# Feed-forward slices taken two at a time, with the weights' lower parts multiplied on 64 rows

## The chip, the core and the metric

The kernel runs on one core of a Trainium2 chip. The metric is the device time of one execution in microseconds (us), and what counts is the median over several executions. Five engines work side by side: TensorE (PE in the profile, its weight loads PEld), VectorE (DVE), ScalarE (ACT), GpSimd (POOL) and SyncE (SP, which here issues the DMA transfers). Each works through its own list of instructions in order and waits on semaphores for the others.

## The reference

An attention by way of 49 agents in each of 4 batches, and behind it a feed-forward with a sigmoid gate:

```python
# q, k, v: (4, 12480, 128); agents: (4, 49, 128); w_in: (128, 2048); w_out: (2048, 128)
a2k = sm(agents, k)                      # softmax over the keys, scale 1/sqrt(128)
agent_v = a2k @ v                        # (49, 128) in each batch
q2a = sm(q, agents)                      # softmax over the 49 agents
x = (q2a @ agent_v).reshape(49920, 128)
h = x @ w_in
out = (h * (1 / (1 + exp(-1.702 * h)))) @ w_out
```

## The kernel before, in words

`agent_weights` multiplies `agent_v` and `w_in` once for each batch, so that the up projection of the feed-forward is a product of the 49 softmax weights of a token with a matrix of 49 rows and 2048 columns. To keep precision beyond one pass of TensorE, numbers are held as a sum of two parts, a high one (rounded to the type `fp32r`) and a low one, the rest. The matrix becomes `wh` and `wl`. Its 49 rows stand twice in it, at partitions 0 to 48 and at 64 to 112 (`H` = 64).

Tokens go in groups of 960 (`GT`), 13 groups (`NG`) in each of 4 batches: 52 groups. A group has two chunks of 480 tokens (`CH`), and for each chunk `query_pairs` makes one tile of 128 partitions, which holds both parts of the softmax weights. In `sa` (chunk 0) the high parts lie at partitions 0 to 63 and the low parts at 64 to 127. In `sb` (chunk 1) it is the other way round: low parts at 0 to 63, high parts at 64 to 127. One matmul of `wh` with `sa` on 128 rows so sums high times high and high times low.

The hidden width of 2048 is cut in 16 slices of 128 (`NF`). A step `t` of the main loop is one slice of one group:

- `up` makes four matmuls into two PSUM banks `ph` (pool `ps_h`, four banks, so two slices' worth): `wh` with `sa`, `wh` with `sb` (line 362), then `wl` with `sa`, `wl` with `sb` (line 364). ACT then computes two gelus into `g` (line 369; three buffers). `gh`, the rounded copy of `g`, is made by ACT in even slices (`HI_ON_ACT`, line 371) and by DVE in odd ones (line 373), and DVE subtracts for `gl` (line 374). `gh` and `gl` have `LAG + 1`, five, buffers.
- `down`, for the slice four steps back (`LAG` = 4), makes six matmuls with `wo_h` and `wo_l` (line 385) that accumulate over the 16 slices in two banks `po`. Behind the last slice `store` copies them out by ACT and issues two DMAs on SP.

Around this, at fixed steps of each group, stand the side jobs: loads of queries, keys and values, the splitting of keys and queries into bfloat16 parts by POOL (lines 167 to 169), the scores (lines 182 to 189), the softmax of the next group's queries (line 328 is its exponential on ACT, with a table load before it and one back for the gelu), their transposes (line 345), and, for the next batch, key scores, their maximum (`key_max`, with transposes at lines 235 and 241), exponentials and the sum over values (`key_matmuls`, line 272). `beside` lists the jobs for the next batch. They are written ahead of the `up` of their step.

The order written is not quite the order that runs: a planner goes through the program when it is built, with costs of its own for each instruction, and may put an instruction that it holds ready ahead of one that it holds blocked. So in some slices the four up matmuls don't stand in a row.

Of the kernel before, what the change touches and what calls it, by code (L numbers as in the profile page):

```python
# [8 lines left out]
F32 = mybir.dt.float32  # L9
F32R = mybir.dt.float32r  # L10
# [3 lines left out]
AF = mybir.ActivationFunctionType  # L14
# [3 lines left out]
P = 128  # L18
TB = 120
KB = 8  # L20
CH = 480
GT = 2 * CH
LAG = 4
# [14 lines left out]
HI_ON_ACT = (0, 2, 4, 6, 8, 10, 12, 14)  # L38
# [4 lines left out]
def kernel(  # L43
# [10 lines left out]
    nc = tc.nc  # L54
# [3 lines left out]
    NF = F // P  # L58
    NG = N // GT
    NKG = N // (TB * KB)  # L60
    H = P // 2
# [7 lines left out]
    gpool = ctx.enter_context(tc.tile_pool(name="gpool", bufs=3))  # L69
    ps_h = ctx.enter_context(tc.tile_pool(name="ps_h", bufs=4, space=bass.MemoryType.PSUM))  # L70
    ps_o = ctx.enter_context(tc.tile_pool(name="ps_o", bufs=1, space=bass.MemoryType.PSUM))
    ps_m = ctx.enter_context(tc.tile_pool(name="ps_m", bufs=2, space=bass.MemoryType.PSUM))

# [1 line left out]
    ag_sb = const.tile([P, B, A], F32, name="ag_sb")  # L75
    nc.sync.dma_start(out=ag_sb, in_=agT)

    ident = const.tile([P, P], F32, name="ident")
    make_identity(nc, ident)
    # sel[k, m] = 1 where k and m name the same agent in either half  # L80
    sel = const.tile([P, P], F32, name="sel")
    nc.vector.memset(sel, 0.0)
    for c in range(2):
        nc.vector.tensor_add(
            out=sel[:, c * H : c * H + A], in0=ident[:, 0:A], in1=ident[:, H : H + A]
# [5 lines left out]
    for i in range(2):  # L91
        t = const.tile([P, KB, P], F32R, name=f"e_pair{i}")
        nc.gpsimd.memset(t.bitcast(F32), 0.0)
        e_pair.append(t)
        t = const.tile([P, KB, 2 * C + 2], F32R, name=f"v_pair{i}")
        nc.gpsimd.memset(t[:, :, 2 * C :].bitcast(F32), 1.0)
        v_pair.append(t)
        t = const.tile([P, CH // TB, P], F32, name=f"p_pad{i}")
# [7 lines left out]
    part_max = const.tile([P, NKG, A], F32, name="part_max")  # L106
    max_b = const.tile([P, A], F32, name="max_b")

    # a float64's words, low then high, to the nearest float32; what is under
    # float32's range becomes zero and what is over it infinite  # L110
    def load_words(src, i):
        w = loads.tile([P, 512, 2], U32, name="words", tag="kv")
        nc.sync.dma_start(out=w.rearrange("p n w -> p (n w)"), in_=src[:, i * 1024 : (i + 1) * 1024])
# [2 lines left out]
    def to_float32(w, out=None):  # L116
        lo = w[:, :, 0]
        hi = w[:, :, 1]
        ts = nc.vector.tensor_scalar
        stt = nc.vector.scalar_tensor_tensor  # L120
        # 2 ** exponent, with the sign
        tmp = work.tile([P, 2, 512], U32, name="tmp", tag="rest")
        ex = tmp[:, 0].bitcast(I32)
        ts(out=ex.bitcast(U32), in0=hi, scalar1=20, scalar2=0x7FF, op0=ALU.logical_shift_right, op1=ALU.bitwise_and)
        ts(out=ex, in0=ex, scalar1=1023 - 127, scalar2=1023 + 128, op0=ALU.max, op1=ALU.min)
        ts(out=ex, in0=ex, scalar1=float(127 - 1023), scalar2=float(1 << 23), op0=ALU.add, op1=ALU.mult)
        stt(out=ex.bitcast(U32), in0=hi, scalar=0x80000000, in1=ex.bitcast(U32), op0=ALU.bitwise_and, op1=ALU.bitwise_or)
        # the mantissa's upper 45 bits as a whole number, rounded once
        m = work.tile([P, 512], U32, name="m21", tag="o")
        r = tmp[:, 1]  # L130
        ts(out=m, in0=hi, scalar1=0xFFFFF, scalar2=0x100000, op0=ALU.bitwise_and, op1=ALU.bitwise_or)
        ts(out=r, in0=lo, scalar1=8, scalar2=None, op0=ALU.logical_shift_right)
        stt(out=m.bitcast(F32), in0=m, scalar=float(1 << 24), in1=r, op0=ALU.mult, op1=ALU.add)
        if out is None:
            out = m.bitcast(F32)
        stt(out=out, in0=m.bitcast(F32), scalar=2.0**-44, in1=ex.bitcast(F32), op0=ALU.mult, op1=ALU.mult)
        return out
# [7 lines left out]
        nc.scalar.copy(out=wo_h[:, s, :], in_=wo)  # L145
        nc.vector.tensor_sub(out=wo_l[:, s, :], in0=wo, in1=wo_h[:, s, :].bitcast(F32))

    # ---- scores: a float32 is the sum of three bfloat16, and of the parts'
    # products all are summed but those under a float32 product's own rounding ----
    ag_part = const.tile([P, B, 3, A], BF16, name="ag_part")  # L150
    rest = ag_sb
    for i in range(3):
# [7 lines left out]
        w = t.bitcast(BF16).rearrange("p (n w) -> p n w", w=2)  # L160
        return w[:, :, 1], w[:, :, 0]

    # the upper half of a word is the first part; of what is left the upper
    # half is the second, and the third takes the place of the lower
    def split(t):
        r = work.tile([P, GT + PAD], F32, name="rest", tag="rest")
        nc.gpsimd.memset(t[:, GT:], 0.0)  # L167
# [23 lines left out]
                nc.scalar.copy(out=o, in_=s[:, :, 0, :])  # L191
                nc.vector.tensor_add(out=o, in0=s[:, :, 1, :], in1=o)

# [1 line left out]
    def key_load(b, g):  # L195
        t = loads.tile([P, GT + PAD], F32, name="kt", tag="kv")
        nc.sync.dma_start(out=t[:, 0:GT], in_=kT[b, :, g * KB : (g + 1) * KB, :].rearrange("p j t -> p (j t)"))
        return t

    def first_key_scores(g, kt):  # L200
        # two batches' agents to a pass, as many columns as keep the clock up
        for c in range(2):
            ps = ps_m.tile([P, 512], F32, name="ps_m")
            for j in range(KB // 2):
                nc.tensor.matmul(  # L205
                    out=ps[:TB, j * 2 * A : (j + 1) * 2 * A],
                    lhsT=kt[:, c * KB // 2 + j, :],
                    rhs=ag_sb[:, 0:2, :].rearrange("p b a -> p (b a)"),
                    start=True,
                    stop=True,  # L210
                )
            s = ps[:TB, : KB * A].rearrange("p (j b a) -> p j b a", b=2, a=A)[:, :, 0, :]
            i = 2 * g + c
            nc.scalar.copy(out=score[:TB, i * KB // 2 : (i + 1) * KB // 2, :], in_=s)
        nc.vector.tensor_reduce(
            out=part_max[:TB, g, :],
            in_=score[:TB, g * KB : (g + 1) * KB, :].rearrange("p j a -> p a j"),
            axis=AX.X,
            op=ALU.max,
        )  # L220
# [87 lines left out]
            nc.vector.tensor_sub(out=wl[:, s], in0=pw, in1=wh[:, s].bitcast(F32))  # L308
        return wh, wl

# [1 line left out]
    def query_load(b, g):  # L312
        t = loads.tile([P, GT + PAD], F32, name="qt", tag="qt", bufs=2)
        nc.sync.dma_start(out=t[:, 0:GT], in_=qT[b, :, g * GT : (g + 1) * GT])
# [38 lines left out]
        nc.vector.tensor_sub(out=sb[0:H], in0=ps[H:P, :CH], in1=sb[H:P].bitcast(F32))  # L353
        return sa, sb

# [1 line left out]
    def up(f, wts, pairs):  # L357
        wh, wl = wts
        s = slice(f * P, (f + 1) * P)
        ph = [ps_h.tile([P, 512], F32, name="ph") for _ in range(2)]  # L360
        for c in range(2):
            nc.tensor.matmul(out=ph[c][:, :CH], lhsT=wh[:, s], rhs=pairs[c], start=True, stop=False)  # L362
        for c in range(2):
            nc.tensor.matmul(out=ph[c][:, :CH], lhsT=wl[:, s], rhs=pairs[c], start=False, stop=True)  # L364
        g = gpool.tile([P, 2, CH], F32, name="g")
        gh = gpool.tile([P, 2, CH], F32R, name="gh", bufs=LAG + 1)
        gl = gpool.tile([P, 2, CH], F32R, name="gl", bufs=LAG + 1)
        for c in range(2):
            nc.scalar.activation(out=g[:, c, :], in_=ph[c][:, :CH], func=AF.Gelu_apprx_sigmoid)  # L369
        if f in HI_ON_ACT:  # L370
            nc.scalar.copy(out=gh, in_=g)  # L371
        else:
            nc.vector.tensor_copy(out=gh, in_=g)  # L373
        nc.vector.tensor_sub(out=gl, in0=g, in1=gh.bitcast(F32))  # L374
        return gh, gl

    def down(f, gp, po):
        gh, gl = gp
        for lhsT, rhs, first, last in (
            (wo_h, gh, True, False),  # L380
            (wo_h, gl, False, False),
            (wo_l, gh, False, True),
        ):
            for c in range(2):
                nc.tensor.matmul(  # L385
                    out=po[c][:, :CH],
                    lhsT=lhsT[:, f, :],
                    rhs=rhs[:, c, :],
                    start=(f == 0 and first),
                    stop=(f == NF - 1 and last),  # L390
                )
# [5 lines left out]
            t0 = b * N + g * GT + c * CH  # L397
            nc.sync.dma_start(out=outT[:, t0 : t0 + CH], in_=o)

# [1 line left out]
    kts = {}  # L401
    vts = {}
    qts = {}
# [4 lines left out]
    wts = {}  # L408
    pairs = {}
# [41 lines left out]
    def do_weights(b):  # L451
        wts[b] = agent_weights(accs.pop(b))

    # the first batch's keys and values have nothing to run beside, and lie
    # where the weights and the hidden values come to lie afterwards
    def first_keys():
        tags = [("g", 3), ("gh", LAG + 1), ("gl", LAG + 1)]
        tiles = []
# [17 lines left out]
    words = [load_words(w_out, i) for i in range(NF // 4)]  # L476
# [7 lines left out]
    for g in range(NKG):  # L484
# [3 lines left out]
        for j in range(KB):  # L488
            nc.tensor.matmul(
                out=acc_ps[:A, : C + 1],  # L490
                lhsT=score[:TB, g * KB + j, :],
                rhs=vt[:TB, j, :],
                start=(g == 0 and j == 0),
                stop=(g == NKG - 1 and j == KB - 1),
# [10 lines left out]
    do_weights(0)  # L505
    down_weights(0, words[0])

    # what is done for the next batch beside a group: in steps of the group's
    def beside(b, g):
        jobs = {}  # L510
        if b == 0 and g == 0:
# [25 lines left out]
    steps = B * NG * NF  # L537
    live = {}
    po = {}
    for t in range(steps + LAG):  # L540
        n, f = divmod(t, NF)
        if t < steps:
            b, g = divmod(n, NG)
            if f == 0:
                jobs = beside(b, g)
            if f == 0:
                do_query_load(n + 2)
                if n == 0:
                    do_query_split(1)
            if f == QS_AT:  # L550
                do_query_split(n + 2)
            if f == Q_AT:
                do_query_scores(n + 1)
            if f == E_AT:
                do_query_softmax(n + 1)
            for job in jobs.get(f, ()):
                job()
            if f == P_AT:
                do_query_pairs(n + 1)
            live[t] = up(f, wts[b], pairs[n])  # L560
            if f == NF - 1:
                pairs.pop(n)
        if t >= LAG:
            n, f = divmod(t - LAG, NF)
            if f == 0:
                po[n] = [ps_o.tile([P, 512], F32, name=f"po{c}") for c in range(2)]
            down(f, live.pop(t - LAG), po[n])
            if f == NF - 1:
                store(*divmod(n, NG), po.pop(n))

# [37 lines left out]
```

## Time and profile before

| | |
|---|---|
| median of 3 runs | 2139.7 us (2138.86 to 2140.49) |
| span of the profiled execution | 2139.6 us, 0.1 under the median |
| mean granted clock of TensorE | 0.992 |
| PE busy | 2083.2 us (97%) |
| PE weight loads busy | 1777.1 us (83%) |
| DVE busy | 1865.0 us (87%) |
| ACT busy | 1611.9 us (75%) |
| POOL busy | 519.8 us (24%) |
| HBM | 50 GB/s over the span |

The profile is of one execution. It gives no time of that execution apart from its span, from the first instruction to the last, so the span stands for its own time. Matmuls follow one another as in a pipeline, and the ends of their records are modelled: a busy PE may still have room, and the distance between the starts of two matmuls is the surer measure. A row of a group gives the line, the engine, the operation, output and inputs with their shapes, and the count; behind the bar stand the busy time, the mean of one in ns, and the idle time just before them with what ended it. A row of the timeline gives start and duration in us, engine, line and operation; in brackets stand the idle time before it and what ended that.

### The profile page before, as it was taken

How to read it: one execution, taken by the hardware profiler on the slowest of the kernel's cores; microseconds unless marked ns; L12 is line 12 of the kernel's file. 1: busy time of each engine (PE TensorE's matmuls, PEld its weight loads, DVE VectorE, ACT ScalarE, POOL GpSimd, SP SyncE). 2: the span in 40 equal slices, each digit the busy share in tenths (PEclk: the TensorE clock that was granted, in tenths of full speed). 3: DMA queues.
4: the chain of work that ended last, by engine and by line, in shares of the span. 5: the costliest groups of instructions: out<-in, count | busy, mean ns of one | idle time of the engine just before them, and what ended most of it. 6: DMA issues, size and time to landing. Idle time of an engine off the chain costs nothing.

```text
span 2139.6 us, 31613 instructions
## 1 busy us (share of the span) xinstructions
PE 2083.2 (97%) x12232; PEld 1777.1 (83%) x12232; DVE 1865.0 (87%) x2142; ACT 1611.9 (75%) x2590; POOL 519.8 (24%) x383
## 2 busy tenths in 40 slices
PE   8889989999999999999999999999999999999999
PEld 8678878888888887788888888778888888888887
DVE  6998998999889899899888899899898887888876
ACT  3567768977777776987777777798777877778786
POOL 4143445121123433421113342531110101001000
PEclk9999999999999999999999999999999999999999
DMA  9411221211111212112101212111100101010000
GB/s 265 119 48 49 65 73 38 61 48 50 38 38 47 66 47 56 47 56 56 56 20 47 63 49 56 55 51 53 47 19 19 38 19 38 19 38 20 25 14 19
DMA packets 49339, 108.57 MB, mean 51 GB/s; under 512 B 4252, under 2 KB 30172, under 8 KB 49188
## 3 DMA queue, kind: packets, MB, share of 16 engines
q1 hardware_dynamic: 49188, 106.55, 17.2%
q8 instruction: 96, 1.57, 0.3%
q14 instruction: 55, 0.45, 0.1%
HBM read 80.97 MB, written 25.56 MB: 50 GB/s over the span
## 4 chain that ended last, share of the span: by engine, by line
PE 81%; DVE 11%; issue 3%; ACT 3%; POOL 1%; DMA 1%; ACTq 0%; SPq 0%; DVEq 0%; POOLq 0%
PE po L385 43%; PE ph L362 15%; PE ph L364 14%; DVE gl L374 5%; DVE gh L373 2%; PE ps_m L272 1%; PE ps_m L182 1%; PE ps_m L184 1%; POOL score L251 1%; PE ps_m L205 1%; ACT g L369 1%; PE ps_m L345 1%; PE ps_m L306 1%; PE ps_m L183 1%; PE ps_m L185 1%
## 5 line engine op out<-in xcount | busy, mean ns | idle before, releaser
L374 DVE TENSOR_TENSOR gl<-g,gh 128x960 fp32r<-128x960 f32 x832 | 1034.4, 1258 | 189.4 <-ACT gh L371 174.3
L369 ACT ACTIVATE g<-ph 128x480 f32<-128x480 f32 x1664 | 855.2, 573 | 380.5 <-PE ph L364 265.7
L385 PE MATMUL po<-gl,wo_h 128*128 128x480 f32 x1664 | 501.9, 382 | 5.4 <-DVE gl L374 5.4
L385 PE MATMUL po<-gh,wo_h 128*128 128x480 f32 x1664 | 506.1, 383 | 0.7 <-ACT gh L371 0.7
L385 PE MATMUL po<-gh,wo_l 128*128 128x480 f32 x1664 | 501.6, 383 | 0.0
L371 ACT CAST gh<-g 128x960 fp32r<-128x960 f32 x416 | 416.0, 1000 | 10.9
L385 PEld LDWEIGHTS po<-gl,wo_h 128*128 128x128 f32 x1664 | 313.1, 189 | 60.0 <-DVE gl L374 9.2
L385 PEld LDWEIGHTS po<-gh,wo_h 128*128 128x128 f32 x1664 | 313.5, 189 | 53.2 <-ACT gh L371 1.1
L385 PEld LDWEIGHTS po<-gh,wo_l 128*128 128x128 f32 x1664 | 313.8, 189 | 49.9
L362 PE MATMUL ph<-sa,wh 128*128 128x480 f32 x832 | 332.5, 400 | 4.8 <-ACT g L369 4.8
L364 PE MATMUL ph<-sa,wl 128*128 128x480 f32 x832 | 319.3, 384 | 0.0
L362 PE MATMUL ph<-sb,wh 128*128 128x480 f32 x832 | 318.8, 383 | 0.0
L364 PE MATMUL ph<-sb,wl 128*128 128x480 f32 x832 | 316.6, 381 | 0.0
L373 DVE CAST gh<-g 128x960 fp32r<-128x960 f32 x416 | 298.6, 718 | 7.0 <-ACT g L369 6.6
L167 POOL MEMSET qt<- 128x8 f32 x52 | 5.7, 110 | 939.2 <-PE ps_m L185 472.0
L169 POOL TENSOR_TENSOR rest<-rest 128x968 bf16<-128x968 f32 x91 | 188.6, 2072 | 7.1
L362 PEld LDWEIGHTS ph<-sa,wh 128*128 128x128 f32 x832 | 157.7, 190 | 31.7 <-ACT g L369 10.8
L362 PEld LDWEIGHTS ph<-sb,wh 128*128 128x128 f32 x832 | 158.0, 190 | 26.6 <-ACT g L369 6.2
L364 PEld LDWEIGHTS ph<-sb,wl 128*128 128x128 f32 x832 | 156.9, 189 | 25.6 <-issue 1.0
L364 PEld LDWEIGHTS ph<-sa,wl 128*128 128x128 f32 x832 | 157.1, 189 | 24.7 <-issue 1.0
L168 POOL TENSOR_TENSOR rest<-qt 128x968 f32<-128x968 f32 x52 | 110.7, 2129 | 167.8 <-DMA qt<-qT 110.8
L184 PE MATMUL ps_m<-ag_part,rest 128*128 128x98 bf16 x728 | 110.2, 205 | 0.0
(103 smaller groups left out, 2077.8 us busy)
## 6 DMA issues: line engine op xcount, KB each, us to landing
kt<-kT SPq DMA_DIRECT2D x52, 480.0 KB, 3.6
qt<-qT SPq DMA_DIRECT2D x52, 480.0 KB, 3.8
vt<-v SPq DMA_DIRECT2D x52, 480.0 KB, 4.3
outT<-o SPq DMA_DIRECT2D x104, 240.0 KB, 2.2
words<-w_in SPq DMA_DIRECT2D x4, 512.0 KB, 10.9
words<-w_out SPq DMA_DIRECT2D x4, 512.0 KB, 8.2
ag_sb<-agT SPq DMA_DIRECT2D x1, 98.0 KB, 2.1
```

What stands on the lines that cost most here:

```text
L168: nc.gpsimd.tensor_sub(out=r, in0=t, in1=halves(t)[0])
L169: nc.gpsimd.tensor_sub(out=halves(r)[1], in0=r, in1=halves(r)[0])
L182: mm(out=o, lhsT=x0[:, t], rhs=a[:, 0 : 2 * A], start=True, stop=False)
L183: mm(out=o[:, A:], lhsT=x0[:, t], rhs=a[:, 2 * A :], start=False, stop=False)
L184: mm(out=o, lhsT=x1[:, t], rhs=a[:, 0 : 2 * A], start=False, stop=False)
L362: nc.tensor.matmul(out=ph[c][:, :CH], lhsT=wh[:, s], rhs=pairs[c], start=True, stop=False)
L364: nc.tensor.matmul(out=ph[c][:, :CH], lhsT=wl[:, s], rhs=pairs[c], start=False, stop=True)
L369: nc.scalar.activation(out=g[:, c, :], in_=ph[c][:, :CH], func=AF.Gelu_apprx_sigmoid)
L371: nc.scalar.copy(out=gh, in_=g)
L373: nc.vector.tensor_copy(out=gh, in_=g)
L374: nc.vector.tensor_sub(out=gl, in0=g, in1=gh.bitcast(F32))
L385: nc.tensor.matmul(out=po[c][:, :CH], lhsT=lhsT[:, f, :], rhs=rhs[:, c, :], start=(f == 0 and first), stop=(f == NF - 1 and last),)
```

## The change

Two steps of the main loop are now done as a pair, `t0` and `t0 + 1`. The side jobs of both steps are written first, then one call of `up` for both slices, then the two `down`s for the slices four steps back.

`up` takes four `ph` banks at once and first makes the four matmuls with `wh`, on 128 rows as before. The four with `wl` then run on 64 rows: for chunk 0 on partitions 0 to 63, and for chunk 1 on partitions 64 to 127, each with a `tile_position` on that half of TensorE's array. These are the partitions that hold the high parts of `sa` and `sb`; the product of the low part of the weights with the low part of the softmax weights is no longer computed. After them come the four gelus, and then the copies and subtractions of both slices. The numbers of buffers (`ps_h` 4, `g` 3, `gh` and `gl` 5) stay as they are. Comments were removed as well.

```diff
-    def up(f, wts, pairs):
+    def up(f0, wts, pairs):
         wh, wl = wts
-        s = slice(f * P, (f + 1) * P)
-        ph = [ps_h.tile([P, 512], F32, name="ph") for _ in range(2)]
-        for c in range(2):
-            nc.tensor.matmul(out=ph[c][:, :CH], lhsT=wh[:, s], rhs=pairs[c], start=True, stop=False)
-        for c in range(2):
-            nc.tensor.matmul(out=ph[c][:, :CH], lhsT=wl[:, s], rhs=pairs[c], start=False, stop=True)
-        g = gpool.tile([P, 2, CH], F32, name="g")
...
+        fs = (f0, f0 + 1)
+        ph = {}
+        for f in fs:
+            for c in range(2):
+                ph[f, c] = ps_h.tile([P, 512], F32, name="ph")
+                nc.tensor.matmul(
+                    out=ph[f, c][:, :CH], lhsT=wh[:, f * P : (f + 1) * P], rhs=pairs[c], start=True, stop=False
+                )
+        for f in fs:
+            for c in range(2):
+                r = slice(c * H, (c + 1) * H)
+                nc.tensor.matmul(
+                    out=ph[f, c][:, :CH],
+                    lhsT=wl[r, f * P : (f + 1) * P],
+                    rhs=pairs[c][r],
+                    start=False,
+                    stop=True,
+                    tile_position=(c * H, 0),
+                )
+        out = []
+        for f in fs:
+            g = gpool.tile([P, 2, CH], F32, name="g")
+            for c in range(2):
+                nc.scalar.activation(out=g[:, c, :], in_=ph[f, c][:, :CH], func=AF.Gelu_apprx_sigmoid)
+            out.append(g)
+        for i, f in enumerate(fs):
...
+            out[i] = (gh, gl)
+        return out
...
-    for t in range(steps + LAG):
-        n, f = divmod(t, NF)
-        if t < steps:
+    for t0 in range(0, steps + LAG, 2):
+        for t in (t0, t0 + 1):
+            n, f = divmod(t, NF)
+            if t >= steps:
+                break
...
-            live[t] = up(f, wts[b], pairs[n])
-            if f == NF - 1:
+        n, f = divmod(t0, NF)
+        if t0 < steps:
+            live[t0], live[t0 + 1] = up(f, wts[n // NG], pairs[n])
+            if f == NF - 2:
                 pairs.pop(n)
-        if t >= LAG:
-            n, f = divmod(t - LAG, NF)
+        for t in (t0 - LAG, t0 + 1 - LAG):
+            if t < 0:
+                continue
+            n, f = divmod(t, NF)
...
-            down(f, live.pop(t - LAG), po[n])
+            down(f, live.pop(t), po[n])
```

More of the change, by code (lines that the diff above doesn't have):

```diff
@@ L354, in query_pairs @@
         return sa, sb
-    def up(f, wts, pairs):
+    def up(f0, wts, pairs):
         wh, wl = wts
-        s = slice(f * P, (f + 1) * P)
-        ph = [ps_h.tile([P, 512], F32, name="ph") for _ in range(2)]
-        for c in range(2):
-            nc.tensor.matmul(out=ph[c][:, :CH], lhsT=wh[:, s], rhs=pairs[c], start=True, stop=False)
-        for c in range(2):
-            nc.tensor.matmul(out=ph[c][:, :CH], lhsT=wl[:, s], rhs=pairs[c], start=False, stop=True)
-        g = gpool.tile([P, 2, CH], F32, name="g")
[L366 to L375, printed above, removed]
+        fs = (f0, f0 + 1)
[24 more added lines that the diff above has]
+        for i, f in enumerate(fs):
+            g = out[i]
+            gh = gpool.tile([P, 2, CH], F32R, name="gh", bufs=LAG + 1)
+            gl = gpool.tile([P, 2, CH], F32R, name="gl", bufs=LAG + 1)
+            if f in HI_ON_ACT:
+                nc.scalar.copy(out=gh, in_=g)
+            else:
+                nc.vector.tensor_copy(out=gh, in_=g)
+            nc.vector.tensor_sub(out=gl, in0=g, in1=gh.bitcast(F32))
+            out[i] = (gh, gl)
+        return out
@@ L545 @@
                 jobs = beside(b, g)
-            if f == 0:
                 do_query_load(n + 2)
```

## The prediction

> **What bounds the kernel now.** I read the page first (busy shares, chain), then its groups, then the timeline of an ordinary stretch, then the waits.
>
> ```profile
> span 2139.6 us, 31613 instructions
> ...
> PE 2083.2 (97%) x12232; PEld 1777.1 (83%) x12232; DVE 1865.0 (87%) x2142; ACT 1611.9 (75%) x2590; POOL 519.8 (24%) x383
> ...
> PE 81%; DVE 11%; issue 3%; ACT 3%; POOL 1%; DMA 1%; ACTq 0%; SPq 0%; DVEq 0%; POOLq 0%
> ...
> L362 PE MATMUL ph<-sa,wh 128*128 128x480 f32 x832 | 332.5, 400 | 4.8 <-ACT g L369 4.8
> ```
>
> PE is busy 97% and holds 81% of the chain that ended last; PE idles only 4.8 us ahead of the first up matmuls. DVE, at 87%, is close behind. The 832 of the last row is the number of slices, so the change makes 416 pairs. The profiled execution spans 2139.6 us, and the median of the three runs is 2139.7, so the sum can be made against either.
>
> ```profile
> 1500.18 0.39 PE L362 MATMUL ph<-sa,wh 128*128 128x480 f32 x1
> 1500.41 0.38 PE L362 MATMUL ph<-sb,wh 128*128 128x480 f32 x1
> 1500.62 0.38 PE L364 MATMUL ph<-sa,wl 128*128 128x480 f32 x1
> 1500.84 0.38 PE L364 MATMUL ph<-sb,wl 128*128 128x480 f32 x1
> ...
> 1502.38 0.38 PE L362 MATMUL ph<-sa,wh 128*128 128x480 f32 x1
> ...
> 1504.57 0.39 PE L362 MATMUL ph<-sa,wh 128*128 128x480 f32 x1
> ```
>
> ```profile
> 1500.19 0.19 PEld L362 LDWEIGHTS ph<-sb,wh 128*128 128x128 f32 x1
> ```
>
> ```profile
> 1501.04 1.03 ACT L369 ACTIVATE g<-ph 128x480 f32<-128x480 f32 x2
> 1503.23 1.04 ACT L369 ACTIVATE g<-ph 128x480 f32<-128x480 f32 x2 [1.15 <-PE ph L364]
> 1504.29 0.99 ACT L371 CAST gh<-g 128x960 fp32r<-128x960 f32 x1
> ```
>
> ```profile
> 1505.32 1.16 DVE L374 TENSOR_TENSOR gl<-g,gh 128x960 fp32r<-128x960 f32 x1 [1.36 <-ACT gh L371]
> ```
>
> These are rows of the timeline (start, duration), engine by engine. Matmul records last 0.38 us, but starts are 0.22 apart: two slices of ten matmuls run from 1500.18 to 1504.57, so 0.2195 each. The next weight load (PEld) starts 0.01 after the matmul before it, and is hidden by it. A matmul's price is this 0.22, not 0.38.
>
> **The change part by part.** Per pair it keeps four full up matmuls and twelve down matmuls. Four full low matmuls (0.88 us) become four on 64 rows, A0, B0, A1, B1, with A on rows 0-63 and B on rows 64-127. They drop products and load half the rows, but still stream 480 columns each, so they save time only if an A and a B run at once: at best two pitches, 0.44 us a pair, 183 us in all. Against that stands the passage between 128 rows and 64, made twice a pair. The kernel has four matmuls on under 64 rows, the transposes of the key maximum (L241, 49 rows), and beside them the transposes of L235 on 120 rows and 49 columns:
>
> ```profile
> 328.72 0.19 PEld L364 LDWEIGHTS ph<-sb,wl 128*128 128x128 f32 x1
> 329.24 0.13 PEld L241 LDWEIGHTS ps_m<-ident,mrow 49*120 49x120 f32 x1 [0.33 <-PE ph L364]
> 329.43 0.30 PEld L385 LDWEIGHTS po<-gh,wo_h 128*128 128x128 f32 x2
> ```
>
> ```profile
> 328.94 0.37 PE L364 MATMUL ph<-sb,wl 128*128 128x480 f32 x1
> ```
>
> ```profile
> 328.78 0.21 DVE L239 COPY mrow<-mcol 49x120 f32<-49x120 f32 x1
> ```
>
> ```profile
> 1372.79 0.23 DVE mrow L239
> ```
>
> ```profile
> 1373.12 0.13 PEld L241 LDWEIGHTS ps_m<-ident,mrow 49*120 49x120 f32 x1 [3.83 <-issue]
> ```
>
> ```profile
> 1368.34 0.12 PEld L235 LDWEIGHTS ps_m<-ident,mx 120*49 120x49 f32 x1
> 1368.56 0.19 PEld L362 LDWEIGHTS ph<-sa,wh 128*128 128x128 f32 x1
> 1368.67 0.19 PEld L362 LDWEIGHTS ph<-sb,wh 128*128 128x128 f32 x1
> ```
>
> *Entry.* L241's input was ready at 328.99 (328.78 + 0.21). On an idle PE its load starts 0.10 after that (in the chain 1372.79 + 0.23 = 1373.02, load at 1373.12), so 329.09 was due. It started at 329.24, 0.30 after the last full matmul (328.94), where the usual distance is 0.01. That is 0.08 more than the pitch of the matmul in front of it: the array is first emptied. *Exit.* After L241 the next full load comes 0.19 after its load, though its 49 columns take some 0.02 at the pitch of 480 columns in 0.22: the same wait. L235, narrow in columns but on full rows, shows none of it: the load behind it starts at 1368.56, one pitch (0.22) after its own.
>
> The Trainium skill, "TensorEngine Tiling (Array Packing)", Key Properties, says that changing the tiling mode drains TensorE. By that rule alone L235 should have been delayed too, and it was not; with L241 the trace agrees, 0.30 instead of 0.01. The section gives no price; by its rule the sum below is the same, with L235 as the exception.
>
> Once emptied, the array also lacks its weights. In the last fence two loads follow 0.11 apart (1368.56, 1368.67), the second when the first's matmul has really begun: 0.11 from load to matmul. A passage costs 0.30 + 0.11 = 0.41 between matmul starts instead of 0.22.
>
> *The sum for PE, from the start T of a pair's last full up matmul.* A0 at T + 0.41. B0's load comes 0.11 behind A0's, and no two loads of this type above are closer, so B0 at 0.52. Each half's next matmul is a pitch later: A1 0.63, B1 0.74. Exit 0.41: the first down matmul at 1.15. Before, it came five pitches after T, 1.10. So +0.05 a pair; unrounded 1.15 - 1.0975 = 0.0525, times 416 is **+22 us**. The overlap is eaten by the two passages. Bounds: A and B loading side by side give 1.04, a gain of 0.0575 or 24 us; no overlap at all gives 0.41, 0.63, 0.85, 1.07 and 1.48, a loss of 0.3825 or 159 us. I take the value between, as its rows are all measured.
>
> *Banks.* Four ph banks stay, now filled by one pair. Before, a slice's gelus start at 1501.04 and end at 1502.07, and its banks are taken again at 1504.57: 2.5 us to spare. After, with a pair's start as 0, A0 runs at 0.66 + 0.41 = 1.07, ACT starts 0.42 later (1500.62 to 1501.04), and four gelus at 0.52 end at 3.57; the fourth bank is wanted at 4.39 + 0.05 + 0.66 = 5.10. To spare: 1.53, so 1 us less, and the down matmuls of that time are used up. What is late next is ACT:
>
> ```profile
> 1510.91 1.28 ACT L328 ACT_TABLE_LOAD   x1
> 1512.20 0.53 ACT L328 ACTIVATE sd<-sd 120x392 f32<-120x392 f32 x1
> 1512.75 1.28 ACT L369 ACT_TABLE_LOAD   x1
> ```
>
> ```profile
> ACT g L369 <- DVE gl L374: 92.3, 74, 2.8
> ...
> PEld ph L362 <- ACT g L369: 17.0, 58, 2.0
> ...
> PE ph L362 <- ACT g L369: 4.8, 6, 1.6
> ```
>
> The waits' columns are total, times and longest. Each of the 52 query groups (4 batches of 13) holds ACT for 3.1 us. By bare slack PE should lose 3.1 - 2.5 = 0.6 each today, 31 us; the waits show 17.0 + 4.8 = 21.8, or 0.7 of it. After, 3.1 - 1.53 = 1.57 each, 82 us, times 0.7 is 57, so **+35 us**. Low bound 0 (scores and key matmuls fill PE); high bound 92, if all of ACT's waits for gl reach PE as well.
>
> *Hidden buffers.* g has three buffers, so a pair's second gelus wait for gl of the pair before's first slice. That slice's copy now follows all four gelus: 3.57 + 0.99, then gl 1.16 ends at 5.72; wanted at 1.49 + 4.44 + 1.04 = 6.97, 1.25 to spare. Before: gl ends at 1506.48, wanted three slices on, at 1503.23 + 6.58 = 1509.81, 3.3 to spare. Covered at nothing on average; uncovered it is the 92 just named. gh and gl have five buffers where six slices are live: the second gh waits for the first down of its iteration, done near 1.81 + 1.31 + 0.17 = 3.3, before its gelus end at 3.57: nothing. Instruction counts on ACT, DVE, POOL and SP, and their DMAs, stay. The side jobs come out in front of a pair, not of a slice, so those at odd steps move one up matmul group earlier, and the last pair ends with its activations together, at most a slice later (2 us): zero taken.
>
> Sum: 2139.6 + 22 + 35 = **2197 us**. This case's own range is 2116 (side by side, no stalls) to 2254 (22 + 92).
>
> **The rivals.**
>
> *No emptying for these matmuls (faster).* L235 speaks for it, and L241 is a transpose of plain float32, seen at entry once behind a busy PE. Then A0 0.22, B0 0.33, A1 0.44, B1 0.55, down at 0.77: 0.33 a pair, -137 us; with the 35 us of stalls 2038, with one passage of the two still dear about 2117. It decides once a passage costs under 0.12 us extra: (0.33 - 35/416) / 2. Against it: the 0.30 at 329.24, with its input ready 0.15 before it could be used. Beyond this DVE's 87% would become the limit.
>
> *Loads side by side.* 2139.6 - 24 + 35 = 2151. No row here has two row halves, so nothing excludes it; against it stands the 0.11 between loads. The Trainium skill, "TensorE: Matmul & The Clock Gate", Part 3, The mechanism, lets loads of different row groups overlap and has matmuls of different tiles start about 4 ns apart. No run here shows it.
>
> *The change doesn't do what it says (slower).* Halves run one after the other, or other work is put between an A and its B: 2139.6 + 159 + 35 = 2334. For it: a row of this kernel with two matmuls streaming at once does not exist.
>
> **How the numbers follow.** Main case 0.42 (2197), side by side 0.17 (2151), no emptying 0.22 (2038), no overlap 0.19 (2334). About 0.2%, 4.3 us, is what a measurement can tell from no change. Faster: nearly all of 0.22, and 0.05 from the low ends of the first two, 0.27; same 0.06; slower 0.67. The range, 2035 to 2320, leaves out half of each outer rival, some 0.2.
>
> **What would show it.** Emptying: the load of the first 64-row matmul 0.3 after the last full one, and of the first down matmul 0.3 after B1. Overlap: B0's start 0.1 behind A0's and A1's 0.22 behind A0's; 0.22 between each would be no overlap. Stalls: PE's wait for g well over 21.8, at the table loads. ACT's wait for gl rises from 92.3. If the first down matmul comes 0.8 after the last full one, I am wrong on the emptying, and if PE's idle time does not rise, on the banks.

## The result, and the profile after

The change made the kernel slower: a median of 2223.3 us (2222.2 to 2226.7), against 2139.3 us before, a ratio of 1.0393 [1.0379, 1.0407], so +84 us. The prediction was 2197 us, within 2035 to 2320.

The page of the kernel after, its head, and the engines' share of the chain that ended last:

```profile
span 2220.9 us, 31819 instructions
...
PE 2160.5 (97%) x12232; PEld 1590.1 (72%) x12232; DVE 1862.6 (84%) x2142; ACT 1573.6 (71%) x2596; POOL 534.1 (24%) x383
...
PE 73%; DVE 15%; ACT 6%; issue 4%; DMA 1%; POOL 1%; ACTq 0%; SPq 0%; DVEq 0%; POOLq 0%
```

PE is still shown 97% busy, with as many matmuls, but its busy time grew by 77.3 us although half of the low matmuls were to be hidden. In the chain DVE has gone from 11% to 15% and ACT from 3% to 6%. Its waits (total, times, longest) say where to look:

```profile
PEld ph L372 <- issue: 166.9, 542, 0.8
...
PEld po L406 <- issue: 142.1, 453, 0.6
...
ACT g L384 <- DVE gl L394: 79.0, 60, 3.8
...
PEld ph L364 <- ACT g L384: 51.4, 119, 2.1
...
PE ph L364 <- ACT g L384: 15.4, 26, 1.7
```

Two things are new. The first two rows are the emptying of the array, once ahead of a 64-row matmul and once behind one: 309 us of waits of the weight loads, with 542 entries where 416 pairs need 416. The last two are PE's waits for gelus, 66.8 us where they were 21.8.

A pair as it was meant, on the timeline of the kernel after, matmuls first, then weight loads (start, duration):

```profile
1759.24 0.38 PE L364 MATMUL ph<-sb,wh 128*128 128x480 f32 x1
1759.55 0.48 PE L372 MATMUL ph<-sa,wl 64*128 64x480 f32 x1
1759.56 0.48 PE L372 MATMUL ph<-sb,wl 64*128 64x480 f32 x1
1759.88 0.37 PE L372 MATMUL ph<-sa,wl 64*128 64x480 f32 x1
1759.88 0.38 PE L372 MATMUL ph<-sb,wl 64*128 64x480 f32 x1
1760.19 0.71 PE L406 MATMUL po<-gh,wo_h 128*128 128x480 f32 x2
```

```profile
1759.55 0.18 PEld L372 LDWEIGHTS ph<-sa,wl 64*128 64x128 f32 x1 [0.34 <-issue]
1759.55 0.18 PEld L372 LDWEIGHTS ph<-sb,wl 64*128 64x128 f32 x1
1759.66 0.19 PEld L372 LDWEIGHTS ph<-sa,wl 64*128 64x128 f32 x1
1759.66 0.19 PEld L372 LDWEIGHTS ph<-sb,wl 64*128 64x128 f32 x1
1760.19 0.30 PEld L406 LDWEIGHTS po<-gh,wo_h 128*128 128x128 f32 x2 [0.34 <-issue]
```

The last full matmul starts at 1759.24, and the loads of A0 and B0 both come 0.31 later. They take 0.11: the next two loads, which follow when A0 and B0 have begun, start at 1759.66. A1 and B1 run one pitch after that, at 1759.88, together; 0.31 after them comes the load of the first down matmul, which so begins at 1760.30. That is 1.06 us for what took 1.10 before (1.0975 unrounded): a whole block gains a little, 0.04.

A pair that was not left whole, in the same kernel, matmuls only:

```profile
422.01 0.38 PE L364 MATMUL ph<-sa,wh 128*128 128x480 f32 x1
422.32 0.48 PE L372 MATMUL ph<-sa,wl 64*128 64x480 f32 x1
422.73 0.48 PE L364 MATMUL ph<-sb,wh 128*128 128x480 f32 x1
423.14 0.48 PE L372 MATMUL ph<-sb,wl 64*128 64x480 f32 x1
423.55 0.49 PE L406 MATMUL po<-gh,wo_h 128*128 128x480 f32 x1
```

Each low matmul runs alone between two passages, so each start is 0.41 behind the one before, not 0.22. From the first row to the first down matmul (423.55 + 0.11) it is 1.65 us where four pitches are 0.88: 0.38 lost for each single low matmul. In the order of the built program, 338 of the 416 pairs have their four low matmuls in a row. The planner broke up the other 78, into 153 ones, 54 twos and 17 threes.

### The profile page after: what moved, and what is told of

Its sections match the earlier page's. It is cut to its first block, busy times and chain, and to the rows that moved or that the text cites. A ratio compares the mean times of both kernels' runs of the same rounds, so it can differ in the third digit from the quotient of the medians.

```text
span 2220.9 us, 31819 instructions
## 1 busy us (share of the span) xinstructions
PE 2160.5 (97%) x12232; PEld 1590.1 (72%) x12232; DVE 1862.6 (84%) x2142; ACT 1573.6 (71%) x2596; POOL 534.1 (24%) x383
## 4 chain that ended last, share of the span: by engine, by line
PE 73%; DVE 15%; ACT 6%; issue 4%; DMA 1%; POOL 1%; ACTq 0%; SPq 0%; DVEq 0%; POOLq 0%
PE po L406 41%; PE ph L364 14%; PE ph L372 11%; DVE gl L394 8%; ACT g L384 3%; ACT gh L391 2%; DVE gh L393 1%; PE ps_m L272 1%; PE ps_m L205 1%; PE ps_m L182 1%; PE ps_m L184 1%; POOL score L251 1%; PE ps_m L345 1%; PE ps_m L306 1%; DVE sd L322 1%
## 5 line engine op out<-in xcount | busy, mean ns | idle before, releaser
L384 ACT ACTIVATE g<-ph 128x480 f32<-128x480 f32 x1664 | 834.5, 574 | 536.0 <-PE ph L372 418.5
L394 DVE TENSOR_TENSOR gl<-g,gh 128x960 fp32r<-128x960 f32 x832 | 1056.7, 1305 | 58.8 <-ACT gh L391 56.8
L406 PE MATMUL po<-gh,wo_h 128*128 128x480 f32 x1664 | 548.1, 410 | 0.0
L406 PEld LDWEIGHTS po<-gh,wo_h 128*128 128x128 f32 x1664 | 284.6, 190 | 157.6 <-issue 131.6
L364 PE MATMUL ph<-sa,wh 128*128 128x480 f32 x832 | 336.8, 405 | 16.2 <-ACT g L384 15.4
L372 PE MATMUL ph<-sb,wl 64*128 64x480 f32 x832 | 313.1, 441 | 0.0
L372 PE MATMUL ph<-sa,wl 64*128 64x480 f32 x832 | 308.0, 438 | 0.0
L372 PEld LDWEIGHTS ph<-sa,wl 64*128 64x128 f32 x832 | 127.4, 185 | 145.9 <-issue 144.8
L169 POOL TENSOR_TENSOR rest<-rest 128x968 bf16<-128x968 f32 x91 | 206.7, 2272 | 7.1
L372 PEld LDWEIGHTS ph<-sb,wl 64*128 64x128 f32 x832 | 128.6, 185 | 22.1 <-issue 22.1
L168 POOL TENSOR_TENSOR rest<-qt 128x968 f32<-128x968 f32 x52 | 99.8, 1919 | 160.2 <-DMA qt<-qT 125.2
```

Source lines behind the costliest of these rows:

```text
L168: nc.gpsimd.tensor_sub(out=r, in0=t, in1=halves(t)[0])
L169: nc.gpsimd.tensor_sub(out=halves(r)[1], in0=r, in1=halves(r)[0])
L364: nc.tensor.matmul(out=ph[f, c][:, :CH], lhsT=wh[:, f * P : (f + 1) * P], rhs=pairs[c], start=True, stop=False)
L372: nc.tensor.matmul(out=ph[f, c][:, :CH], lhsT=wl[r, f * P : (f + 1) * P], rhs=pairs[c][r], start=False, stop=True, tile_position=(c * H, 0),)
L384: nc.scalar.activation(out=g[:, c, :], in_=ph[f, c][:, :CH], func=AF.Gelu_apprx_sigmoid)
L406: nc.tensor.matmul(out=po[c][:, :CH], lhsT=lhsT[:, f, :], rhs=rhs[:, c, :], start=(f == 0 and first), stop=(f == NF - 1 and last),)
```

## The experiments

The theory behind the first runs was the prediction's: passages, plus PE's waits for late gelus. The rivals were that the loss lies in one of the two alone, that the halves need their matmuls alternated, that broken pairs carry the loss, and that buffers of `g`, not banks, carry the stalls. Medians and ratios to the kernel before:

| run | us | ratio [95%] | PE's waits for gelus, us |
|---|---|---|---|
| before | 2139.3 | | 17.0 + 4.8 |
| after | 2223.3 | 1.0393 [1.0379, 1.0407] | 51.4 + 15.4 |
| pair_full | 2190.6 | 1.0233 [1.0208, 1.0258] | 55.4 + 18.1 |
| single_64 | 2265.0 | 1.0583 [1.0556, 1.0610] | 8.0 + 1.4 |
| halves_apart | 2214.0 | 1.0336 [1.0310, 1.0362] | 39.5 + 8.9 |
| held | 2208.7 | 1.0312 [1.0283, 1.0341] | 86.5 + 47.1 |
| held_full | 2203.6 | 1.0312 [1.0296, 1.0327] | 75.7 + 40.9 |
| no_exp_before | 2123.7 | 0.9932 [0.9915, 0.9948] | 3.4 + 1.6 |
| no_exp_after | 2163.8 | 1.0123 [1.0108, 1.0138] | 44.3 + 24.6 |
| g4 | 2177.6 | 1.0178 [1.0153, 1.0203] | 14.1 + 0.4 |
| g4_full | 2153.4 | 1.0073 [1.0057, 1.0088] | 10.5 + 0.7 |
| g4_held | 2161.5 | 1.0111 [1.0097, 1.0124] | 16.8 + 3.6 |
| g4_held_full | 2165.2 | 1.0119 [1.0102, 1.0136] | 13.8 + 6.3 |
| g4_before | 2126.9 | 0.9948 [0.9936, 0.9961] | 8.9 + 1.6 |

The last column adds the waits of PEld and PE as the prediction did. The two overlap in part, so it is an index of stalls, not a sum that adds up to the loss.

### The two parts of the change apart

**pair_full**: two slices at a time, low matmuls on 128 rows.

```diff
-                    lhsT=wl[r, f * P : (f + 1) * P],
-                    rhs=pairs[c][r],
+                    lhsT=wl[:, f * P : (f + 1) * P],
+                    rhs=pairs[c],
...
-                    tile_position=(c * H, 0),
```

> The changed kernel with its four low matmuls of a pair on 128 rows again; pairs, buffers and the order of PE's instructions are the changed kernel's, so only the 64 rows are undone. Theory (passages): whole blocks of four 64-row matmuls gain 0.0575 us each as they stand (338 of them, 19 us), but the planner left 153 single 64-row matmuls, 54 twos and 17 threes, and each such fragment pays two passages: a single 0.82 instead of 0.44 us, a two 0.82 instead of 0.66. That is +58, +9 and about +2, so +50 us net for the 64 rows, and without them the time is about 2173 us: 35 above the kernel before, by waits for banks. Rival (stalls): the whole loss of 84 us is waits for the four banks that a pair takes at once, the 64 rows are neutral, and the time stays at about 2220 us.

Measured 2190.6, +52 us, between the theory's 2173 and the rival's 2220. The built order of PE is the same as after's, so after minus pair_full, +33, is what the 64 rows cost there. The waits of pair_full:

```profile
ACT g L378 <- DVE gl L388: 140.8, 106, 3.8
...
PEld ph L364 <- ACT g L378: 55.4, 125, 2.2
...
PEld po L400 <- DVE gl L388: 19.9, 7, 3.2
...
PE ph L364 <- ACT g L378: 18.1, 23, 1.8
```

PE's waits for gelus rise by 52, from 21.8 to 73.5, and above them ACT waits for `gl` 106 times, for the `g` buffer that `gl` has not yet read, where before it was 74 times. PE also waits for `gl` itself, ahead of down matmuls: 19.9 + 17.1 us, where before it was 9.2 + 5.4. One stall of the first kind, on the timeline of pair_full, by ACT, DVE and the weight loads:

```profile
820.39 1.03 ACT L378 ACTIVATE g<-ph 128x480 f32<-128x480 f32 x2 [3.04 <-DVE gl L388]
```

```profile
816.15 1.02 DVE L189 TENSOR_REDUCE score<-ps_m 120x196 f32<-120x392 f32 x2
...
818.54 0.69 DVE L267 CAST v_pair<-vt 120x1024 fp32r<-120x1024 f32 x1
819.14 2.22 DVE L388 TENSOR_TENSOR gl<-g,gh 128x960 fp32r<-128x960 f32 x2
```

```profile
821.01 0.19 PEld L364 LDWEIGHTS ph<-sa,wh 128*128 128x128 f32 x1 [1.51 <-ACT g L378]
```

DVE does work on scores, keys and values from 816.15 to 819.14, with one copy of `gh` between. The first of the two `gl` then ends near 820.3. ACT, which has sat idle 3.04 us for that buffer, starts its gelus at 820.39; PE, whose bank those gelus empty, stands for 1.51. No table load is in it.

**single_64**: before, slice by slice, with its two low matmuls on 64 rows.

```diff
         for c in range(2):
-            nc.tensor.matmul(out=ph[c][:, :CH], lhsT=wl[:, s], rhs=pairs[c], start=False, stop=True)
+            r = slice(c * H, (c + 1) * H)
+            nc.tensor.matmul(
+                out=ph[c][:, :CH], lhsT=wl[r, s], rhs=pairs[c][r], start=False, stop=True, tile_position=(c * H, 0)
+            )
```

> The kernel before, slice by slice, with its two low matmuls of a slice on 64 rows. Bank and buffer use stay as before. Theory (passages): a two comes at 0.41 us behind the last full matmul and the next full one 0.41 behind that, 0.82 instead of 0.66, on 788 twos 127 us, and on 84 singles 0.38 each, 32 us: about 2298 us. Rival (stalls): without pairs no waits for banks, and the overlap of the halves shows as a gain: under 2139 us.

Measured 2265.0, +126.5 us. A slice on the timeline of its matmuls:

```profile
1753.67 0.38 PE L362 MATMUL ph<-sb,wh 128*128 128x480 f32 x1
1753.98 0.49 PE L365 MATMUL ph<-sa,wl 64*128 64x480 f32 x1
1753.99 0.49 PE L365 MATMUL ph<-sb,wl 64*128 64x480 f32 x1
1754.40 0.69 PE L388 MATMUL po<-gh,wo_h 128*128 128x480 f32 x2
```

Two passages for one overlapped pair of matmuls: with 0.41 at either end, 0.82 where three pitches took 0.66. That is 0.16 for each of 788 slices whose low matmuls stand together, 126 us. The 84 singles of the other slices were expected to add 32, and the total stays 33 under the theory's 2298. PE runs its matmuls in the same order as in the kernel before, so the two traces can be set side by side, start by start: the twos cost 126 us and the singles some 34, but all other distances between matmuls are 32 shorter in sum. PE's waits for gelus, 12 lower by the table, are a part of that.

### How the halves run

**halves_apart**: after, with both low matmuls of chunk 0 listed ahead of both of chunk 1 (A0, A1, B0, B1).

```diff
-        for f in fs:
-            for c in range(2):
+        for c in range(2):
+            for f in fs:
                 r = slice(c * H, (c + 1) * H)
```

> The changed kernel with the four 64-row matmuls of a pair in the order A0, A1, B0, B1 instead of A0, B0, A1, B1; all else is the same. Theory (matmuls start in the order of the list, and only neighbours on different halves overlap): A0 at 0.41, A1 and B0 at 0.63, B1 at 0.85, the next at 1.26 instead of 1.04, so 0.22 on each of 338 whole blocks, 74 us: about 2297 us. Rival (each half has a queue of its own, or the loads alone set the pace): no change, 2223 us.

Measured 2214.0, so the rival held, and not the theory. Its timeline, matmuls:

```profile
1752.02 0.48 PE L372 MATMUL ph<-sa,wl 64*128 64x480 f32 x1
1752.03 0.49 PE L372 MATMUL ph<-sb,wl 64*128 64x480 f32 x1
1752.35 0.37 PE L372 MATMUL ph<-sa,wl 64*128 64x480 f32 x1
1752.36 0.37 PE L372 MATMUL ph<-sb,wl 64*128 64x480 f32 x1
```

In the order of the built program the two low matmuls on `sa` stand ahead of the two on `sb`. B0, third in that list, starts 0.01 after A0 and 0.32 before A1. The overlap does not depend on an order that alternates. The 9 us under after go with fewer waits for gelus (48.4).

### Pairs kept whole against the planner

**held**: after, with the low matmuls bound behind the last full matmul of their pair and the down matmuls behind the last low one. **held_full**: the same with low matmuls on 128 rows.

```diff
-                nc.tensor.matmul(
+                full = nc.tensor.matmul(
...
-                nc.tensor.matmul(
+                with tc.issue_after(full.ins):
+                  held[0] = nc.tensor.matmul(
...
-            down(f, live.pop(t), po[n])
+            with tc.issue_after(held[0].ins):
+                down(f, live.pop(t), po[n])
```

> The changed kernel with an order on PE laid down when it is built: the low matmuls of a pair behind its last full one, and the down matmuls behind the last low one. The 64-row matmuls then stand in 399 blocks of four and 34 of two, with no singles. Theory (passages): the 70 us of the fragments go, the whole blocks gain 23 us against full matmuls, the twos cost 5, and the waits for banks stay at 35 or grow somewhat, as PE may no longer do down matmuls while a bank is late: 2150 to 2180 us. Rival (stalls): holding the order turns the planner's way around late banks into waits, and the time rises above 2223 us.

> The kernel with the order on PE laid down (held), with its low matmuls on 128 rows again; the order on PE is that of held. Theory (a whole block of four 64-row matmuls is a small gain): held has 399 whole blocks, 0.0575 us each or 23 us, and 34 twos at 0.16, 5 us, so 128 rows are 18 us slower here: about 2226 us. Rival (the 64 rows cost time in whole blocks too, as the main case of the prediction had it): about 20 us faster, near 2188 us.

Measured 2208.7 and 2203.6: neither theory's numbers, and the two can't be told apart (both ratios are 1.0312). The waits of held:

```profile
PEld po L409 <- issue: 137.7, 414, 0.6
PEld ph L375 <- issue: 130.1, 413, 0.8
...
PEld ph L366 <- ACT g L387: 86.5, 132, 4.2
...
PE ph L366 <- ACT g L387: 47.1, 50, 3.8
```

The blocks are whole (399 of 416), the entries fall from 542 to 413 and the emptying from 309 to 268 us. But the waits for gelus double, from 66.8 to 133.6. The order does that by itself: on 128 rows, held_full waits 116.6 against pair_full's 73.5 and takes 13 us more. The planner had broken pairs where gelus were late; an order that forbids it turns the gain into stalls. Start by start, the whole blocks of held gain 15 us on held_full and its twos lose 6, but the other distances are 16 longer. So whole pairs could be judged only with the stalls out of the way.

### What makes the gelus late

**no_exp_before, no_exp_after**: both kernels with their exponentials replaced by scaled copies, so that ACT loads two tables in all, at the start (140 loads in after); the softmaxes are left out.

```diff
-        nc.scalar.activation(out=sc, in_=sc, func=AF.Exp, scale=scale)
+        nc.scalar.activation(out=sc, in_=sc, func=AF.Copy, scale=scale)
...
-        nc.scalar.activation(out=e[:TB], in_=e[:TB], func=AF.Exp, scale=scale)
+        nc.scalar.activation(out=e[:TB], in_=e[:TB], func=AF.Copy, scale=scale)
```

> The kernel before with its two exponentials (queries and keys) replaced by a scaled copy on ACT, so the softmaxes are left out, and with them ACT's table loads. Theory (ACT held at the table loads is what makes banks late): PE's waits for the gelus, 21.8 us now, mostly go: 2110 to 2130 us. Rival (banks are late for other reasons): less than 10 us from 2139.

> The changed kernel with its two exponentials replaced by a scaled copy on ACT, so the softmaxes are left out, and with them ACT's table loads. Theory (pairs have less time to spare, and ACT held for 3 us at the table loads uses it up): nearly all of the 52 us that pairs cost go, and with 391 whole blocks, 39 twos and 22 singles in the order built the 64 rows come out 8 us ahead (23 less 6 and 8): 2105 to 2130 us, level with the kernel before without its exponentials or a little under it. Rival (DVE and the three g buffers are what makes banks late): the gap of 84 us stays by more than half.

Measured 2123.7 and 2163.8. The first is as the theory had it; the second is neither the theory's 2105 to 2130 nor clearly the rival, for the gap between the kernels falls from 84 to 40 us, just under a half. Most of that fall can't be put down to stalls. Without the exponentials the planner builds another order, with 391 pairs whole and 39 twos and 22 ones in the rest. By the prices of this document, an estimate, the whole blocks then gain 15 us and the fragments lose 15, so the 64 rows cost nothing, where they cost 33 in after. That leaves some 11 of the 44 us for what table loads hold up, and PE's waits for gelus in no_exp_after stay at 68.9. Nor do table loads suffice alone, as the last batch of the kernels with exponentials shows. It has query groups with their table loads like the others, but no key work for a next batch beside it. Its first up matmul on the timelines of before, pair_full and after:

```profile
1654.86 0.38 PE L362 MATMUL ph<-sa,wh 128*128 128x480 f32 x1
```

```profile
1699.71 0.38 PE L364 MATMUL ph<-sa,wh 128*128 128x480 f32 x1
```

```profile
1734.89 0.38 PE L364 MATMUL ph<-sa,wh 128*128 128x480 f32 x1
```

To the ends of the spans (2139.6, 2188.1, 2220.9) it is 484.7, 488.4 and 486.0 us. Of the 81 us between the spans of before and after, 80 arise ahead of the last batch. In it all 104 pairs are whole in after, and after takes 2.4 us less than pair_full: the broken pairs, too, all lie ahead of it. Busy times of before, start-up, the first three batches and the last (length, then PE, PEld, DVE, ACT, POOL):

```profile
73.00:1655.00 1582.00, 1545.73 (x9235) 1314.05 (x9234) 1430.40 (x1625) 1216.04 (x1937) 456.14 (x314) 0.99 0.17 49
1655.00:2139.00 484.00, 480.54 (x2537) 410.20 (x2535) 384.72 (x434) 376.71 (x608) 37.58 (x30) 1.00 0.08 25
```

DVE is 90% busy in the three batches that lose (1430.40 of 1582.00) and 79% in the one that doesn't. The page's average, 87%, hides both.

**g4**: after with four buffers of `g` (to make room, the second `p_pad` is the first one). **g4_full**: the same with low matmuls on 128 rows, in the same built order.

```diff
-            g = gpool.tile([P, 2, CH], F32, name="g")
+            g = gpool.tile([P, 2, CH], F32, name="g", bufs=4)
```

> The changed kernel with four buffers for g instead of three; the room comes from one p_pad instead of two. Theory (banks and ACT, not buffers): the order built has 114 singles instead of 153, 39 x 0.38 us or 15 us less, and nothing else changes: about 2208 us. Rival (gelus wait for a g buffer, as a pair takes two of three at once): most of the 52 us that pairs cost go, and the time falls to 2160 to 2175 us.

> Pairs with four g buffers and the low matmuls on 128 rows; the order on PE is that of g4. Theory (the three g buffers are what pairs cost, passages are what 64 rows cost): in g4's order 353 whole blocks gain 20 us, 114 singles lose 43 and 39 twos 6, so without 64 rows the time is 29 us lower than g4's 2178: about 2149 us, 10 over the kernel before. Rival (pairs go on costing their 52 us by banks, and g4 won by its order alone): about 2190 us.

Measured 2177.6 (its runs spread from 2168.5 to 2180.2), 46 us below after and near the rival's 2160 to 2175, and 2153.4, 37 below pair_full and near the theory's 2149. The waits of g4:

```profile
PEld ph L373 <- issue: 161.0, 506, 0.8
...
PEld ph L365 <- ACT g L385: 14.1, 55, 0.6
...
ACT g L385 <- DVE gl L395: 6.8, 6, 1.9
```

ACT's waits for `gl` fall from 79.0 to 6.8 and PE's for gelus from 66.8 to 14.5. The four `ph` banks are unchanged, and the table loads are in: the stalls were the third buffer's. Some 15 of the 46 us, an estimate, go with the order built, which has 114 ones instead of 153; the 37 between the two kernels on 128 rows have no such part, since fragments cost nothing there. What is left in g4 over g4_full, 24 us, is the price of 64 rows with broken pairs (506 entries).

**g4_held, g4_held_full**: g4 and g4_full with the order of held.

> The changed kernel with four g buffers and the order on PE laid down, so 399 whole blocks and 34 twos. Theory (with the buffer the waits for gelus go, 14 us of them in g4, and the whole blocks keep their gain of 23 less 5 us): 2120 to 2140 us, level with the kernel before or below it. Rival (a laid-down order makes PE wait, as held was no faster than with 128 rows): 2160 us or more.

> Pairs with four g buffers, the order on PE laid down as in g4_held, and the low matmuls on 128 rows. It prices whole blocks of four 64-row matmuls with waits for gelus out of the way (g4_held: 2161.5). Theory (a whole block gains 0.0575 us): 399 blocks less 34 twos are 18 us, so 128 rows are slower: about 2179 us. Rival (what PE gains in a block it gives back, in later waits or in granted clock, 0.982 in g4_held's profile): within 6 us of 2161, or below it.

Measured 2161.5 and 2165.2, so the theories (2120 to 2140 and 2179) failed and the rivals held. Whole blocks are 16 us better than the planner's mixture (g4), but against 128 rows in the same order they are 4 us ahead with intervals that overlap, no difference that can be told. Block by block a gain is there, but smaller than the theories took it. The starts of two groups, with a third between them, in a quiet stretch of g4_held and then of g4_held_full:

```profile
421.14 0.38 PE L367 MATMUL ph<-sa,wh 128*128 128x480 f32 x1
...
497.27 0.38 PE L367 MATMUL ph<-sa,wh 128*128 128x480 f32 x1
```

```profile
419.44 0.38 PE L367 MATMUL ph<-sa,wh 128*128 128x480 f32 x1
...
496.51 0.38 PE L367 MATMUL ph<-sa,wh 128*128 128x480 f32 x1
```

Two groups of eight pairs take 76.13 against 77.07, 0.059 less a pair. That is close to the 0.0575 of the rival "loads side by side", but it is not the gain of a block: in the last batch, read the same way, the groups differ by 0.10 to 0.21 us, 0.01 to 0.03 a pair. The order on PE is the same in both kernels, so all their matmuls can be set side by side, start by start. The distance from the matmul ahead of a whole block to the second one behind it is 0.038 shorter in g4_held (the median of 399 blocks). In sum the whole blocks gain 12.7 us, the 34 twos lose 5.4, and all other distances are 0.6 shorter. That is 8 us, the difference between the two profiled spans:

```profile
core 0: 2156.9 us, clock 0.982
```

```profile
core 0: 2164.8 us, clock 0.986
```

So whole blocks on 64 rows are worth some 13 us in this kernel, and the twos take 5 of them back. The granted clock is lower in g4_held: as an estimate, span times what is missing to 1, it takes 39 us there and 30 in g4_held_full. That does not show as a loss outside the blocks.

**g4_before**: the kernel before with four buffers of `g` and one `p_pad`.

> The kernel before with four g buffers (and one p_pad). Theory: its gelus waited 92 us for a g buffer, but PE waited only 22 us for gelus, so at most those 22 us go: 2120 to 2137 us. Rival (the third buffer hides everything here): 2139 us, no change.

Measured 2126.9, 0.9948 [0.9936, 0.9961]: within the theory's 2120 to 2137, and the one version that beats both kernels with nothing left out. The wait of ACT that the prediction showed with 92.3 us:

```profile
ACT g L370 <- DVE gl L375: 8.0, 5, 2.6
```

It falls to 8.0. Before gains 10 to 12 us by the fourth buffer (2136.9 in the runs beside it, 2139.3 above) and pair_full 37, so with it pairs cost 27 us (2153.4 - 2126.9), not 52. That remainder is not waits for gelus, which are 11.2 and 10.5; by the estimate used above 13 of it would be the granted clock (0.989 against 0.995). It was not followed further.

## Why the prediction was right, and where it was not

**The sum.** Predicted +22 for PE's passages and +35 for stalls; measured +33 (after minus pair_full) and +52 (pair_full minus before). Forecast and side were right, and 2223 lies in the main case's own range, 2116 to 2254. Both terms were low, and both for a reason other than their size alone, so that the sum came within 26 us of 2223 is in part luck.

**Emptying** stood as worked out: 0.30 from the transpose of L241, 0.31 in the kernel after, at both ends, with 0.11 for the load behind it. The rivals without it and without overlap (2038 and 2334) are excluded.

**The load of B0** was the first step to fail. The prediction put it 0.11 behind A0's, the closest that any two loads came in the trace before. Both start at 1759.55, so the first down matmul comes at 1.06 and not at 1.15, and the rival "loads side by side" has the mechanism right: a whole block gains 0.04 (the rival's 0.0575, less 0.01 at each end), not loses 0.05. The Trainium skill, "TensorE: Matmul & The Clock Gate", Part 3, The mechanism, lets loads of different row groups overlap and sets matmuls of different tiles about 4 ns apart. By that rule, the trace agrees: the loads come at one time, and A0 and B0 are recorded 0.01 us apart.

**That every pair is whole** was the second, and it was never written down as a term: "A0, B0, A1, B1" was priced 416 times. The front of the document itself says that in some slices the four up matmuls don't stand in a row. By the prices that the rows give, 338 fours gain 13 us (0.0375), 153 ones lose 58 (0.38), 54 twos 9 (0.16) and the threes some 2 (an estimate): +56, where +33 was measured. The traces of after and pair_full, set side by side start by start, show where the rest went: the whole blocks gain 12 us, the broken pairs lose 53, and all other distances are 9 shorter, together the 32 to 33 us between the two spans. Why the broken pairs lose 53 and not 69 was not taken apart; of the 9, the waits for gelus, 6.7 lower in after, are a part, as if a PE that comes later waited less. So it was chance that the sum for PE, with a loss in whole blocks and none in broken ones, came out near +33.

**Banks.** That pairing uses up slack and PE waits for late gelus was right. The place was not. The step that failed is "Hidden buffers", where three buffers of `g` with 1.25 us to spare were "covered at nothing on average". A stretch of other DVE work ahead of `gl`, 3.0 us in the stall shown, uses that up; of ACT's 140.8 us of waits for `gl` in pair_full, 137.8 fall ahead of the last batch. A fourth buffer took PE's waits to 14.5 in g4 and 37 us off the time of pair_full, with the same four banks, and the 10 to 12 us that it brings to the kernel before leave 25 or more of it to the pairs. The trace had the row for it: ACT's wait for `gl`, 92.3 us and 74 times, was already the largest wait of ACT for a buffer, and the prediction named it as the high bound.

**Table loads** were to be the place of the stalls. Their share is small as far as the runs show it (by estimate some 11 of the 44 us by which the gap falls without them), and the last batch, with its table loads and without key work, loses 1.3 us.

**ACT's wait for gl** was to rise from 92.3. It rose in pair_full, to 140.8, and fell in after, to 79.0, since there PE is late as well: ACT's largest wait for PE, 265.7 before, is 418.5.

## What to carry to other kernels

Price a change of tile shape per passage, not per matmul: here a passage cost 0.19 us beyond a pitch, twice, so two matmuls that overlap with two others just paid for it, one with one lost 0.16, and a lone one lost 0.38. A planner with costs of its own may break the blocks up (78 of 416 pairs here), and binding the order can cost as much in stalls as it saves. When steps are grouped, count each buffer against the longest stretch of other work of the engine that frees it, in the busiest stage and not on average, and try the fourth buffer by itself first: here that alone was worth more than the change.

## What the runs showed of the hardware that was not expected

- Two 64-row halves load their weights at the same time (both loads at 1759.55), and a matmul listed behind another one for the first half starts ahead of it on the second (1752.03 against 1752.35 in halves_apart). The Trainium skill, "TensorE: Matmul & The Clock Gate", Part 3, What overlaps and what doesn't, holds matmuls to the order of the list in start and end; this row differs, and the measurement decides.
- Entering and leaving 64 rows empties the array (0.31 us each), while the transposes of L235 on 49 columns and 120 rows, in the prediction's rows, did not.
- The granted clock went down along with pairs, from 0.992 before to 0.986 after and 0.982 in g4_held, and up in g4_before (0.995) and single_64 (0.993). By the estimate above that is 31 us of after and 17 of before, 14 of the 84. It was neither predicted nor tested, but the trace of after shows what it goes with. The clock falls to 0.50 for stretches of 3.4 us or a multiple, and ahead of nine of the eleven before the end PE was busy for two thirds of the last 3.4 us or less: 0.79 us of them ahead of the drop at 204.6, 1.28 ahead of the one at 1221.8. So PE's long waits may cost a second time.
